# A new order for batch 0's prologue, attention of batch 1 two pieces later, and a later gate on batch 3's loads

## The chip, the cores and the metric

One core of a Trainium2 chip. Times are device microseconds (us) of one execution, medians of several. "Span" is the time of the profiled execution from its first to its last instruction; it is about 2 us shorter than the device time. Engines: PE is TensorE, PEld its weight loads, DVE is VectorE, ACT is ScalarE, POOL is GpSimd, SP is SyncE (SPq its queue of DMA issues). L571 is line 571 of that kernel; the changed kernel's lines are off by one here and there.

## The reference

Attention with projected keys and values (8 batches, 8 heads, 1024 positions, head size 64, 64 projected positions), then a maxout of two products, then an output product.

```python
k_proj = np.einsum('ks,bhsd->bhkd', E, k)
v_proj = np.einsum('ks,bhsd->bhkd', F, v)
scores = scale * np.matmul(q, k_proj.transpose(0, 1, 3, 2))
scores = scores - np.max(scores, axis=-1, keepdims=True)
attn = np.exp(scores)
attn = attn / (np.sum(attn, axis=-1, keepdims=True) + 1e-09)
attn_out = np.matmul(attn, v_proj).astype(np.float32)
x = attn_out.transpose(0, 2, 1, 3).reshape(B * S, H * D)
h1 = x @ w1; h2 = x @ w2
return (np.maximum(h1, h2) @ w_out).astype(np.float32)
```

## The kernel before

It uses max(h1, h2) = relu(x (w1 - w2)) + x w2. So it needs wd = w1 - w2 ("up" products, with a relu), m = w2 w_out (from transposes of w2, `step_w2t`, and `step_m`), and "down" products of the relu with w_out and of x with m. A batch is two units. From the second batch on, up and down products are cut into seven smaller products each (sums and differences of blocks), and each down product into pieces, between which the attention of later batches is placed. `at_slot(key, step)` hangs a step on a place in that list: ("P", unit, product, piece), ("U", unit, half, product) or ("G", unit, half).

The parts that the change and the argument touch:

```python
    def step_kv(t, h0=0, h1=H, which="kv", att=False, dma=False):   # projection of k and v
        # ... matmuls ...
        if both:                      # which == "v": batch 0's v
            eng = nc.scalar.copy if att else nc.vector.tensor_copy
            eng(out=t["vp"][:, h0:h1], in_=zd(kv_ps[:, 0:n]))
        # ...
    def step_kpt_dma(t):              # transposes projected k, issued by SyncE
        nc.sync.dma_start_transpose(
            out=t["kpt"], in_=t["kp"].rearrange("p h r d -> p (h r d)")
        )

    def step_gate(t, n, *at):         # GpSimd waits here for a tile, then issues the next loads
        nc.gpsimd.tensor_copy(out=junk, in_=t[n][(slice(0, 1), *at, slice(0, 1))])

    def step_qt_dma(t, h0=0, h1=H):   # transposes q, issued by SyncE
        nc.sync.dma_start_transpose(
            out=t["qt"][:, h0:h1].rearrange("q h (i p) -> q (h i) p", p=128),
            in_=t["q"][:, h0:h1].rearrange("p h c d -> p (h c d)"),
        )
    # ... prologue, batch 0, second group of four heads ...
    step_inv(t, 0, 1)
    warm(4)
    step_qt(t, 4, 4, 0, NI // 2)
    step_qt(t, 4, 4, NI // 2, NI)
    warm(2)
    step_sc(t, 1, 0)
    step_sc(t, 1, 1)
    step_kv(t, 0, 4, "v")
    step_dn(t, 1, 0)
    step_at(t, 0, 0)
    step_dn(t, 1, 1)
    step_at(t, 0, 1)
    step_inv(t, 1, 0)
    step_kv(t, 4, 8, "v", True)
    step_inv(t, 1, 1)
    step_wd(0, 0, 2)
    step_at(t, 1, 0, True)
    u0, u1 = [*up_slots(t, 0)], [*up_slots(t, 1)]
    step_wd(0, 2, 4)
    step_at(t, 1, 1, True)
    for u in u0, u1:
        for x in u[0:2]:
            x(r1=2)                   # first halves of four up products
    # ... slots: second halves, further w2 transposes (wt), wd blocks, step_m ...

    t = tiles[2]                      # batch 2
    at_slot(("P", 0, 1, 0), new_attn, t)
    at_slot(("P", 0, 1, 0), step_qt_dma, t, 0, H // 2)
    at_slot(("U", 1, 0, 1), step_kv, t, 0, H, "kv", True)
    at_slot(("U", 1, 0, 4), step_kpt, t, 0, H, True)
    at_slot(("G", 1, 0), step_qt_dma, t, H // 2, H)
    at_slot(("U", 1, 0, 6), step_gate, t, "qt", H // 2 - 1)
    at_slot(("U", 1, 0, 6), loads, 3, "k", "v", "q")

    for b in range(3, B):             # batches 3 to 7
        t = tiles[b]
        n = 2 * b - 3
        key = ("G", n, 0) if b == 3 else ("U", n - 1, 1, 5)
        at_slot(key, new_attn, t)
        at_slot(key, step_qt_dma, t, 0, H // 2)
        at_slot(key, step_qt_dma, t, H // 2, H)
        at_slot(("U", n, 0, 1), step_kv, t, 0, H, "kv", True, True)   # issues step_kpt_dma
        # ... gates and loads of batch b + 1 ...
```

The softmax here doesn't subtract the row's maximum and nothing guards it: scores larger than these inputs give would overflow.

Of the kernel before, what the change touches and what calls it, by code (L numbers as in the profile page):

```python
# [16 lines left out]
def kernel(  # L17
# [161 lines left out]

    def step_kv(t, h0=0, h1=H, which="kv", att=False, dma=False):  # L180
        kv_ps = att_banks()[:, 0, :] if att else mm_bank()
# [18 lines left out]
        if both:  # L200
            eng = nc.scalar.copy if att else nc.vector.tensor_copy
            eng(out=t["vp"][:, h0:h1], in_=zd(kv_ps[:, 0:n]))
        elif "v" in which:
            def finish_v():
                nc.vector.tensor_copy(out=t["vp"][KP:128, h0:h1], in_=zd(kv_ps[KP:128, 0:n]))
                if dma:
                    nc.vector.tensor_copy(out=kp[:, :, 1, :], in_=kp[:, :, 0, :])
                    step_kpt_dma(t)
                nc.vector.tensor_copy(out=fl(t["vp"][0:KP]), in_=fl(t["vp"][KP:128]))

            if att:
                return finish_v
            finish_v()
# [112 lines left out]

    def step_at(t, g, j, att=False):
        if "xt" not in t:
            new_xt(t)
        ld = t.pop(("ld", g, j))  # L330
        if att:
            both = att_banks()
            at_ps = [both[:, o, :] for o in range(2)]
        else:
            at_ps = [mm_bank() for _ in range(2)]
        values_into(t, g, j, at_ps)
        for o in range(2):
            nc.vector.tensor_tensor(
                out=x_out(t, g, j)[:, :, o, :],
                in0=at_ps[o].rearrange("q (z n) -> q z n", z=2),  # L340
                in1=ld[:, o, None, :].broadcast_to([128, 2, W]),
                op=ALU.mult,
            )
# [91 lines left out]

    def step_w2t(f0):
        ps_t = mm_bank(FP16)
        for f in range(2):
# [11 lines left out]
    def step_m(r):  # L450
        m_ps = mm_bank(n=(1, 2, 0, 3)[r])
        for fb in range(NFB):
# [170 lines left out]
    def down_steps(u, alone):  # L623
# [51 lines left out]

        def keep_d(bank):
            return keep("pd", bank, *([nc.vector.tensor_copy] if u["n"] == 0 else []))

        size = 2 * (NG + NX) // (1 if alone else 2 if u["n"] == 0 else 3)
# [7 lines left out]
        def p1():  # L687
            st["s1"] = keep_d(whole(1, "X", xbank))

# [3 lines left out]
        def p6():  # L693
            st["u1"] = keep_d(whole(6, "X", None))

        def p5():
            st["s5"] = keep_d(whole(5, "Z", ybank))

        def p7():
            st["u2"] = keep_d(whole(7, "X", None))  # L700
            if alone:
                add(1, 1, st["u2"], st["s5"])
# [49 lines left out]
    step_inv(t, 0, 1)  # L752
    warm(4)
    step_qt(t, 4, 4, 0, NI // 2)
    step_qt(t, 4, 4, NI // 2, NI)
    warm(2)
    step_sc(t, 1, 0)
    step_sc(t, 1, 1)
    step_kv(t, 0, 4, "v")
    step_dn(t, 1, 0)  # L760
    step_at(t, 0, 0)
    step_dn(t, 1, 1)
    step_at(t, 0, 1)
    step_inv(t, 1, 0)
    step_kv(t, 4, 8, "v", True)
    step_inv(t, 1, 1)
    step_wd(0, 0, 2)
    step_at(t, 1, 0, True)
    u0, u1 = [*up_slots(t, 0)], [*up_slots(t, 1)]
    step_wd(0, 2, 4)  # L770
    step_at(t, 1, 1, True)
    for u in u0, u1:
        for x in u[0:2]:
            x(r1=2)


# [5 lines left out]
    def loads(b, *names):  # L782
# [16 lines left out]
    slots = [  # L799
        (0, lambda: u0[0](r0=2)), (1, lambda: u0[1](r0=2)), (None, lambda: loads(1, "v", "q", "k")),  # L800
        (2, lambda: u1[0](r0=2)), (3, lambda: u1[1](r0=2)),
        (None, wd[1]), (4, u0[2]), (None, wt[0]), (5, u0[3]),
        (None, wd[2]), (None, wt[1]), (6, u1[2]), (7, u1[3]), (None, wt[2]), (None, wt[3]), (8, u0[4]), (9, u0[5]), (None, wd[3]),
        (10, u1[4]), (11, u1[5]), (12, u0[6]), (13, u0[7]),
# [8 lines left out]
    for n, key in enumerate(units):  # L813
# [6 lines left out]
        ups = [*up_steps(U[units[n + 1]])]  # L820
        for h, (x, y) in enumerate(((5, 1), (1, 2)) if n == 1 else ((2, 2), (2, 3))):
            slots += pieces[:x]
# [27 lines left out]
    for n, x in enumerate((  # L850
        "", "", "kv", "", "kpt", "qt00 qt10", "", "sc00 sc10", "qt01", "qt11", "",
        "dn00 in00 dn10 in10", "", "", "at00 AT10 sc01",
    )):
        key = ("P", 0, (n - 1) // 2, (n - 1) % 2) if n else (0, 19)
        for name in x.split():
# [18 lines left out]
    t = tiles[2]  # L874
    at_slot(("P", 0, 1, 0), new_attn, t)
    at_slot(("P", 0, 1, 0), step_qt_dma, t, 0, H // 2)
    at_slot(("U", 1, 0, 1), step_kv, t, 0, H, "kv", True)
    at_slot(("U", 1, 0, 4), step_kpt, t, 0, H, True)
    at_slot(("G", 1, 0), step_qt_dma, t, H // 2, H)
    at_slot(("U", 1, 0, 6), step_gate, t, "qt", H // 2 - 1)  # L880
    at_slot(("U", 1, 0, 6), loads, 3, "k", "v", "q")
# [22 lines left out]
    for n, (b, o) in enumerate(units):  # L904
        u = U[b, o]

        if b == 0:
            where = ()
        elif n == 2:
            where = (("P", 1, 0, 2), 0), (("P", 1, 1, 0), 1), (("P", 1, 1, 1), 2), (("U", 1, 0, 1), 3)  # L910
        else:
            where = tuple((("U", n - 2, 1, k), i) for k, i in ((6, 2), (3, 0), (4, 1), (5, 3)))
# [49 lines left out]
```

## Time and profile before

| | before |
|---|---|
| device time, median of 6 runs | 325.81 us (325.12 to 327.21) |
| span of the profiled execution | 323.2 us |
| PE, DVE, ACT, POOL busy | 316.0, 236.8, 203.1, 41.6 us |

PE is busy 98% of the span: only its waits can be won. The prediction shows the lines on which it rests. Those of the stage that also belong here are GpSimd's and SyncE's timelines around batch 3's loads, in the kernel before. Columns: start, duration, engine, line, what it does, and in brackets how long the engine was idle before it and what ended that.

```profile
71.82 0.61 POOL L238 COPY junk<-qt_sb 1x1 f16<-1x1 f16 x1 [19.08 <-DMA qt_sb<-q_sb]
73.04 0.90 POOL L102 DMA_DIRECT2D k_sb<-in_k_dram  x1 [0.62 <-PE mm_ps L571]
83.40 0.87 POOL L102 DMA_DIRECT2D v_sb<-in_v_dram  x1 [9.46 <-DMA qt_sb<-q_sb]
84.27 0.88 POOL L102 DMA_DIRECT2D q_sb<-in_q_dram  x1
```

```profile
100.17 5.70 SPq L258 DMA_TRANSPOSE qt_sb<-q_sb  x2
105.96 0.53 SPq L664 DMA_DIRECT2D out_dram<-o_sb  x1
106.97 1.20 SPq L232 DMA_TRANSPOSE kpt_sb<-kp_sb  x1
```

The first fence: the gate passes at 71.82, when batch 2's first q transpose has landed, and k's load goes out at 73.04. v and q go out 10 us later, since v's load itself waits for the second q transpose (the bracket says so). The second fence: q has landed at 84.27 + 15.8 = 100.07 (15.8 is the tile view's time from issue to landing), SyncE's queue then issues q's two transposes, a store, and the transpose of projected k (`kpt_sb`). This lands 2.7 us after its issue, at 109.7; PE's scores of batch 3 want it at 110.2.

### The profile page before, as it was taken

Reading aid. Unit: us, or ns where it says so; the run is one execution under the profiler, and the core shown is the slowest. Engines: PE = TensorE matmul, PEld = TensorE weight load, DVE = VectorE, ACT = ScalarE, POOL = GpSimd, SP = SyncE. Lnnn points to the kernel's source line nnn. Section 1 sums busy time; section 2 is a strip of 40 time slices with the busy share of each in tenths; the row PEclk is TensorE's granted clock in tenths of the full one; section 3 lists DMA queues with packets and bytes.
Section 4 is the critical chain, followed back from the end, with each engine's and each line's share of the span. In section 5 each row is a group of like instructions: output and inputs, shape, how many; then the busy total and the mean of one; then the engine's idle time right before and its main releaser. Section 6 shows DMA issues by size and latency. Waiting matters only on the chain.

```text
span 323.2 us, 9033 instructions
## 1 busy us (share of the span) xinstructions
PE 316.0 (98%) x3852; PEld 248.4 (77%) x3852; DVE 236.8 (73%) x420; ACT 203.1 (63%) x364; POOL 41.6 (13%) x65
## 2 busy tenths in 40 slices
PE   8989999999999999999999999999999999999995
PEld 3554457878887888878887888878887888888884
DVE  1365798896867797877967796977967796969572
ACT  1466532667676777667776777657776777764541
POOL 8649002001200300030000300030000000000000
PEclk9999999999999999999999999999999999999999
DMA  8999999999999799699979999689969130312133
GB/s 160 207 196 185 204 204 204 207 203 179 256 216 213 135 203 244 143 177 144 234 147 201 154 211 231 115 180 183 232 130 213 38 100 32 99 34 98 34 121 108
DMA packets 76280, 53.14 MB, mean 164 GB/s; under 512 B 29520, under 2 KB 76112, under 8 KB 76240
## 3 DMA queue, kind: packets, MB, share of 16 engines
q0 software_dynamic: 30976, 28.31, 56.0%
q1 hardware_dynamic: 45264, 24.25, 31.2%
q8 instruction: 30, 0.49, 0.6%
q14 instruction: 10, 0.08, 0.1%
HBM read 57.15 MB, written 16.78 MB: 229 GB/s over the span
## 4 chain that ended last, share of the span: by engine, by line
PE 84%; DMA 9%; DVE 2%; POOL 2%; issue 1%; SPq 1%; ACT 0%; DVEq 0%; POOLq 0%
PE mm_ps L649 43%; PE mm_ps L571 24%; PE att_ps L188 4%; DMA v_sb<-in_v_dram 4%; DMA qt_sb<-q_sb 3%; PE mm_ps L415 3%; PE att_ps L287 3%; PE mm_ps L275 3%; PE mm_ps L453 2%; DMA big<-in_moe_w_dram 2%; POOL q_sb L102 1%; POOL k_sb L102 1%; DVE gt_sb L586 1%; PE mm_ps L246 1%; PE mm_ps L440 1%
## 5 line engine op out<-in xcount | busy, mean ns | idle before, releaser
L542 ACT COPY p_sb<-mm_ps 128x512 f32<-128x512 f32 x172 | 97.2, 594 | 42.0 <-PE mm_ps L571 30.0
L649 PEld LDWEIGHTS <-big 128*128 128x128 f16 x768 | 73.5, 98 | 12.0 <-issue 3.5
L649 PE MATMUL mm_ps<-T_sb,big 128*128 128x256 f16 x576 | 77.9, 273 | 0.0
L586 DVE TENSOR_TENSOR gt_sb<-mm_ps,p_sb 128x512 f16<-128x512 f32 x56 | 38.6, 688 | 45.5 <-PE mm_ps L571 42.7
L571 PE MATMUL mm_ps<-big,big 128*128 128x256 f16 x336 | 50.4, 273 | 0.0
L571 PEld LDWEIGHTS <-big 128*128 128x128 f16 x448 | 43.8, 98 | 5.2
L649 PEld LDWEIGHTS <-gt_sb 128*128 128x128 f16 x384 | 35.8, 98 | 9.9 <-issue 5.4
L649 PE MATMUL mm_ps<-wo_sb,gt_sb 128*128 128x256 f16 x256 | 43.0, 273 | 0.1
L571 PEld LDWEIGHTS <-wd_sb 128*128 128x128 f16 x336 | 32.9, 98 | 3.8
L571 PE MATMUL mm_ps<-xt_sb,wd_sb 128*128 128x256 f16 x224 | 33.6, 273 | 0.0
L364 ACT ACTIVATE ex_sb<-mm_ps 128x512 f16<-128x512 f32 x50 | 27.2, 597 | 10.2 <-PE att_ps L287 8.1
L390 DVE TENSOR_TENSOR xt_sb<-att_ps,ld_sb 128x1024 f16<-128x1024 f32 x26 | 31.7, 1219 | 0.1
L673 DVE TENSOR_TENSOR o_sb<-mm_ps,p_sb 128x512 f32<-128x512 f32 x32 | 21.9, 685 | 7.7 <-PE mm_ps L649 7.7
L649 PE MATMUL mm_ps<-m_sb,xt_sb 128*128 128x256 f16 x128 | 24.4, 273 | 0.0
L238 POOL COPY junk<-qt_sb 1x1 f16<-1x1 f16 x6 | 1.7, 284 | 169.6 <-DMA qt_sb<-q_sb 169.6
L621 ACT ACTIVATE gt_sb<-mm_ps 128x512 f16<-128x512 f32 x28 | 16.8, 600 | 8.7 <-PE mm_ps L571 8.7
L532 DVE TENSOR_TENSOR big<-gt_sb 128x1024 f16<-128x1024 f16 x32 | 21.9, 685 | 0.3
L589 DVE TENSOR_SCALAR gt_sb<-gt_sb 128x512 f16<-128x512 f16 (+1 forms) x56 | 20.4, 365 | 1.9
L649 PE MATMUL mm_ps<-wo_sb,big 128*128 128x256 f16 x128 | 21.5, 273 | 0.0
L649 PE MATMUL mm_ps<-T_sb,gt_sb 128*128 128x256 f16 x128 | 21.5, 273 | 0.0
L649 PEld LDWEIGHTS <-xt_sb 128*128 128x128 f16 x192 | 18.8, 98 | 2.2
L586 DVE TENSOR_TENSOR gt_sb<-p_sb 128x512 f16<-128x512 f32 x28 | 19.1, 682 | 0.0
(88 smaller groups left out, 429.5 us busy)
## 6 DMA issues: line engine op xcount, KB each, us to landing
out_dram<-o_sb SPq DMA_DIRECT2D x63, 256.0 KB, 2.7
k_sb<-in_k_dram POOLq DMA_DIRECT2D x7, 1024.0 KB, 11.3
v_sb<-in_v_dram POOLq DMA_DIRECT2D x7, 1024.0 KB, 16.7
q_sb<-in_q_dram POOLq DMA_DIRECT2D x5, 1024.0 KB, 22.8
q_sb<-in_q_dram POOLq DMA_DIRECT2D x4, 512.0 KB, 19.4
big<-in_moe_w_dram POOLq DMA_DIRECT2D x12, 128.0 KB, 8.6
k_sb<-in_k_dram POOLq DMA_DIRECT2D x4, 256.0 KB, 6.1
q_sb<-in_q_dram POOLq DMA_DIRECT2D x4, 256.0 KB, 7.2
```

The costliest lines, as they stand in the source:

```text
L188: nc.tensor.matmul(out=kv_ps[r * KP : (r + 1) * KP, 0:n], lhsT=eft[:, i, c, :], rhs=t[w][:, h0:h1, c, :], start=(c == 0), stop=(c == NC - 1),)
L275: nc.tensor.matmul(out=banks[e][pos : pos + Z, h * W : (h + 1) * W], lhsT=t["kpt"][o * D : (o + 1) * D, head, s * Z : (s + 1) * Z], rhs=t[ ...
L364: nc.scalar.activation(out=t["ex", g, j][:, e, :], in_=banks[e], func=ACTF.Exp, scale=scale)
L390: nc.vector.tensor_tensor(out=x_out(t, g, j).rearrange("q z o n -> q o z n"), in0=at_ps.rearrange("q o (z n) -> q o z n", z=2), in1=ld[:, ...
L532: nc.vector.tensor_tensor(out=S(i), in0=x, in1=y, op=op)
L542: copy(out=x, in_=bank)
L571: nc.tensor.matmul(out=bank[:, m * W : (m + 1) * W], lhsT=w_[:, n_, (2 * d + m) * 128 : (2 * d + m + 1) * 128], rhs=a[:, n_, :], start=(n ...
L586: nc.vector.tensor_tensor(out=c_blk(j, c), in0=two(x), in1=two(y), op=ALU.add)
L589: nc.vector.tensor_scalar_max(ap, ap, 0.0)
L621: nc.scalar.activation(out=out, in_=in_, func=ACTF.Relu)
L649: nc.tensor.matmul(out=bank[:, i * CH : (i + 1) * CH], lhsT=a(c)[:, i * 128 : (i + 1) * 128], rhs=w_(c), start=(n is not None and m == (lo ...
L673: nc.vector.tensor_tensor(out=o_sb, in0=two(x), in1=two(y), op=ALU.add)
```

## The change

Its intent: in batch 0, do work while the loads of v and w1 are awaited (v's first projection between the two scores, 16 transposes of w2 before the third up product, four warm-up matmuls out); move batch 1's attention two pieces later so that its loads are there; let ScalarE instead of VectorE keep unit 0's partial results; and let batch 2's second q transpose finish before batch 3's loads start.

```diff
@@ step_kv: engine of the copy given by the caller
-            eng = nc.scalar.copy if att else nc.vector.tensor_copy
-            eng(out=t["vp"][:, h0:h1], in_=zd(kv_ps[:, 0:n]))
+            copy(out=t["vp"][:, h0:h1], in_=zd(kv_ps[:, 0:n]))
@@ step_at: a step between its two multiplications; step_w2t: may use the attention's banks (cut)
@@ step_m
-        m_ps = mm_bank(n=(1, 2, 0, 3)[r])
+        m_ps = mm_bank(n=(3, 0, 1, 2)[r])
@@ down_steps, for p1, p6, p5, p7 alike
-        def keep_d(bank):
-            return keep("pd", bank, *([nc.vector.tensor_copy] if u["n"] == 0 else []))
-            st["s1"] = keep_d(whole(1, "X", xbank))
+            st["s1"] = keep("pd", whole(1, "X", xbank))
@@ prologue
-    warm(4)
     step_qt(t, 4, 4, 0, NI // 2)
     step_qt(t, 4, 4, NI // 2, NI)
     warm(2)
     step_sc(t, 1, 0)
+    step_kv(t, 0, 4, "v")
     step_sc(t, 1, 1)
-    step_kv(t, 0, 4, "v")
+    step_at(t, 0, 0)
     step_dn(t, 1, 0)
-    step_at(t, 0, 0)
+    step_at(t, 0, 1, between=lambda: step_wd(0, 0, 2))
     step_dn(t, 1, 1)
-    step_at(t, 0, 1)
+    step_kv(t, 4, 8, "v", copy=nc.scalar.copy)
     step_inv(t, 1, 0)
-    step_kv(t, 4, 8, "v", True)
+    step_at(t, 1, 0, True)
     step_inv(t, 1, 1)
-    step_wd(0, 0, 2)
-    step_at(t, 1, 0, True)
...
             x(r1=2)
+    step_w2t(0, True)
...
         (0, lambda: u0[0](r0=2)), (1, lambda: u0[1](r0=2)), (None, lambda: loads(1, "v", "q", "k")),
+        (None, lambda: step_w2t(256, True)),
         (2, lambda: u1[0](r0=2)), (3, lambda: u1[1](r0=2)),
-        (None, wd[1]), (4, u0[2]), (None, wt[0]), (5, u0[3]),
-        (None, wd[2]), (None, wt[1]), (6, u1[2]), ...
+        (None, wd[1]), (4, u0[2]), (5, u0[3]),
+        (None, wd[2]), (6, u1[2]), ...
@@ pieces of unit 1 around its groups
-        for h, (x, y) in enumerate(((5, 1), (1, 2)) if n == 1 else ((2, 2), (2, 3))):
+        for h, (x, y) in enumerate(((6, 1), (1, 1)) if n == 1 else ((2, 2), (2, 3))):
@@ batch 1's attention: two empty places put in front
-        "", "", "kv", "", "kpt", "qt00 qt10", ...
+        "", "", "", "", "kv", "", "kpt", "qt00 qt10", ...
@@ batch 2
-    at_slot(("P", 0, 1, 0), new_attn, t)
-    at_slot(("P", 0, 1, 0), step_qt_dma, t, 0, H // 2)
+    at_slot(("P", 0, 2, 0), new_attn, t)
+    at_slot(("P", 0, 2, 0), step_qt_dma, t, 0, H // 2)
...
-    at_slot(("U", 1, 0, 6), step_gate, t, "qt", H // 2 - 1)
+    at_slot(("U", 1, 0, 6), step_gate, t, "qt", H - 1)
     at_slot(("U", 1, 0, 6), loads, 3, "k", "v", "q")
```

More of the change, by code (lines that the diff above doesn't have):

```diff
@@ L177, in new_attn, with step_kv @@
         t["qt"] = qtp.tile([128, H, HALF], FP16, tag="qt", name="qt_sb")
-    def step_kv(t, h0=0, h1=H, which="kv", att=False, dma=False):
+    def step_kv(t, h0=0, h1=H, which="kv", att=False, dma=False, copy=nc.vector.tensor_copy):
         kv_ps = att_banks()[:, 0, :] if att else mm_bank()
@@ L325, in step_inv, with step_at @@
         nc.scalar.activation(out=ld, in_=ld, func=ACTF.Exp, scale=-1.0)
-    def step_at(t, g, j, att=False):
+    def step_at(t, g, j, att=False, between=None):
         if "xt" not in t:
@@ L337, in step_at @@
         for o in range(2):
+            if o and between is not None:
+                between()
             nc.vector.tensor_tensor(
@@ L434, in step_wd, with step_w2t @@
         )
-    def step_w2t(f0):
-        ps_t = mm_bank(FP16)
+    def step_w2t(f0, att=False):
+        ps_t = att_banks(FP16)[:, 0, :] if att else mm_bank(FP16)
         for f in range(2):
@@ L693, in p6 @@
         def p6():
-            st["u1"] = keep_d(whole(6, "X", None))
+            st["u1"] = keep("pd", whole(6, "X", None))
         def p5():
-            st["s5"] = keep_d(whole(5, "Z", ybank))
+            st["s5"] = keep("pd", whole(5, "Z", ybank))
         def p7():
-            st["u2"] = keep_d(whole(7, "X", None))
+            st["u2"] = keep("pd", whole(7, "X", None))
             if alone:
@@ L800 @@
         (0, lambda: u0[0](r0=2)), (1, lambda: u0[1](r0=2)), (None, lambda: loads(1, "v", "q", "k")),
+        (None, lambda: step_w2t(256, True)),
         (2, lambda: u1[0](r0=2)), (3, lambda: u1[1](r0=2)),
-        (None, wd[1]), (4, u0[2]), (None, wt[0]), (5, u0[3]),
-        (None, wd[2]), (None, wt[1]), (6, u1[2]), (7, u1[3]), (None, wt[2]), (None, wt[3]), (8, u0[4]), (9, u0[5]), (None, wd[3]),
+        (None, wd[1]), (4, u0[2]), (5, u0[3]),
+        (None, wd[2]), (6, u1[2]), (7, u1[3]), (None, wt[2]), (None, wt[3]), (8, u0[4]), (9, u0[5]), (None, wd[3]),
         (10, u1[4]), (11, u1[5]), (12, u0[6]), (13, u0[7]),
@@ L850 @@
     for n, x in enumerate((
-        "", "", "kv", "", "kpt", "qt00 qt10", "", "sc00 sc10", "qt01", "qt11", "",
+        "", "", "", "", "kv", "", "kpt", "qt00 qt10", "", "sc00 sc10", "qt01", "qt11", "",
         "dn00 in00 dn10 in10", "", "", "at00 AT10 sc01",
     )):
-        key = ("P", 0, (n - 1) // 2, (n - 1) % 2) if n else (0, 19)
+        key = ("P", n // 15, (n - 1) // 2 % 7, (n - 1) % 2) if n else (0, 19)
         for name in x.split():
@@ L909 @@
         elif n == 2:
-            where = (("P", 1, 0, 2), 0), (("P", 1, 1, 0), 1), (("P", 1, 1, 1), 2), (("U", 1, 0, 1), 3)
+            where = (("P", 1, 1, 1), 0), (("P", 1, 1, 2), 1), (("P", 1, 2, 0), 2), (("U", 1, 0, 1), 3)
         else:
```

## The prediction

> **What bounds the kernel now.** I read the page first: its busy shares, its slices, then the chain that ended last.
>
> ```profile
> PE 316.0 (98%) x3852; PEld 248.4 (77%) x3852; DVE 236.8 (73%) x420; ACT 203.1 (63%) x364; POOL 41.6 (13%) x65
> PE   8989999999999999999999999999999999999995
> PE 84%; DMA 9%; DVE 2%; POOL 2%; issue 1%; SPq 1%; ACT 0%; DVEq 0%; POOLq 0%
> ```
>
> TensorE (PE) is busy 316.0 of 323.2 us, so no change that leaves its matmuls alone can win more than about 7 us. Its idle time lies in the first slices and at the end; the end (final add and store) isn't touched. The DMA share of the chain tells where PE waits for data. The chain in order of time, 5 to 30 us:
>
> ```profile
> 8.35 12.82 DMA v_sb<-in_v_dram
> 21.17 0.29 issue
> 21.46 5.01 DMA big<-in_moe_w_dram
> 26.47 0.47 issue
> 26.94 0.70 DVE wd_sb L431
> 27.64 0.05 issue
> 27.69 1.04 PE mm_ps L415 x4
> ```
>
> So the prologue ends on a load: the second half of v, then the last quarter-block of w1 (the tile view gives 5.4 us from its issue at 21.46, so it lands at 26.86), then one subtraction, then the third up product at 27.69. From 27.69 on the matmul starts follow each other without a gap worth naming (switches of tile shape cost 0.1 to 0.2 us each and are in both kernels), except once. The timeline of PE, 16 to 24 us and at 82 us:
>
> ```profile
> 15.57 1.04 PE L148 MATMUL mm_ps<-ones 128*128 128x512 f16 x4
> 18.43 0.41 PE L275 MATMUL att_ps<-qt_sb,kpt_sb 64*32 64x256 f16 x16 [0.16 <-DVE qt_sb L251]
> 18.78 1.06 PE L188 MATMUL mm_ps<-v_sb,eft 128*64 128x256 f16 x16
> 20.36 0.41 PE L287 MATMUL mm_ps<-ex_sb,vp_sb 64*32 64x256 f16 x16 [0.29 <-DVE vp_sb L202]
> 21.22 1.06 PE L188 MATMUL att_ps<-v_sb,eft 128*64 128x256 f16 x16
> 22.75 0.63 PE L287 MATMUL att_ps<-ex_sb,vp_sb 64*32 64x256 f16 x32 [0.47 <-ACT vp_sb L202]
> 23.80 4.92 PE L415 MATMUL mm_ps<-xt_sb,wd_sb 128*128 128x512 f16 x20 [0.42 <-DVE wd_sb L431]
> 82.88 0.41 PE L275 MATMUL mm_ps<-qt_sb,kpt_sb 64*32 64x256 f16 x16 [0.31 <-DMA qt_sb<-q_sb]
> ```
>
> The reader should see four small bracketed waits before 24 us, one more hidden in "4.92 x20" (20 matmuls of 512 columns need 20 x 0.216 = 4.32, so 0.6 is waiting, about half of it for wd at 27.69), and one at 82.88 us. The times 18.78 and 21.22 aren't free: v's first half was issued at 7.59 and took 11.1 us, so it landed at 18.69, and the second landed at 21.17.
>
> **What the Trainium skill says.** "TensorE: Matmul & The Clock Gate", section "Step-by-step: what each phase is for", gives 55.6 ns between starts at 128 columns and about 216 ns at 512. The trace agrees: 16 transposes take 32.04 to 32.94 (56 ns each), 32 matmuls of 512 columns take 6.91 us in the chain (216 ns each). The same page, "What's actually happening", says the clock drops only after an idle window of about 3.4 us; no wait here is near that, and the granted clock is 1.00 in every window I read. "DMA: Bandwidth & Descriptors", section "Issuing engines are not separate DMA queues", says transfers started by different engines run on the same 16 DMA engines and interleave. The trace agrees: the q transpose issued at 66.67 landed in 5.1 us, the one issued at 72.17, with a 1 MB k load issued 0.9 us after it, took 10.7 us.
>
> **The change part by part.**
>
> (a) Four warm-up matmuls at 15.57 go: 0.86 us of PE. But v's first projection now comes after only one block of scores and can't start before 18.7. PE gets there at about 17.4 instead of 18.78 and waits some 1.3 us. Worth nothing.
>
> (b) The second scores of the group move behind that projection. PE: projection 18.77 to 19.77, scores to 20.11; the copy of vp by VectorE (DVE) is done at 20.30 as before, so the wait of 0.29 shrinks, but the values start at 20.36 as before. The exponentials of the moved scores start at 20.25 instead of about 19.3 and take 1.02 (its row at 62.26), so the last sums start at 21.3, and the second projection of v at about 21.64 instead of 21.22. Its copy on ScalarE (ACT) ends at 23.1, the last values start at 23.17 (22.75 before). The first up matmul then starts at about 23.73 (23.80 before: there wd was awaited, and wd is now made one VectorE place earlier).
>
> (c) Two blocks of eight w2 transposes (8 x 0.056 = 0.45 us each) go from behind the 27.69 mark to before it. PE: four half products (8 x 0.216 = 1.73) to 25.46, transposes to 25.91, two halves to 26.77, transposes to 27.22, two halves to 28.08. So the third product starts at 28.08 and not 27.69, but 0.90 us of later work is already done: net 0.90 - 0.39 = 0.51 us won. wd for it is ready at 27.63 as before, so the load is no longer the bound. Had PE been ready by 27.69, the win would be 0.90.
>
> (d) From there PE is continuous, and everything shifts 0.5 us earlier if its data are there. I checked each floor. wd's third block landed at about 30.8 and is subtracted by 31.6; it is wanted at 32.4. w_out landed at 26.72 + 11.3 = 38.0; wanted at 39.3. v of batch 1 landed at 28.64 + 19.5 = 48.1, and the kernel before used it at 48.15, with no slack. A PE 0.5 us earlier would have stopped there. Moving batch 1's attention two pieces later (2 x 6 matmuls x 0.109 = 1.3 us) takes it to about 48.9. This part wins nothing by itself; it keeps the 0.5.
>
> (e) Unit 0's four partial results: VectorE 684 ns each, 2.7 us off an engine that is 86 to 91% busy from 40 to 70 us; ScalarE takes 594 ns each, 2.4 us, where it is only about 30% busy up to 60 us. PE didn't wait for VectorE there, so 0 on the path, but slack.
>
> (f) The gate on batch 3's loads now waits for the second q transpose. That leaves the transpose almost alone: issued at about 72.2, landed at about 77.5 instead of 82.83, wanted at about 82. The wait at 82.88 goes: the gap between starts there was 0.47 against 0.09 at the same switch elsewhere, so 0.38 us won. Batch 3's k goes out at about 77.6 instead of 73.04, v and q earlier than their 83.40; its use is at 102.74.
>
> Sum: 0.51 + 0.38 = 0.9 us off 325.81, so 324.9 us.
>
> **The rivals.**
>
> First, the load is the bound after all and PE is ready by 27.69. For it: my chain in (b) adds several latencies of 0.05 to 0.2 us, and being 0.3 too slow in it is easy. Against it: the moved exponentials really are on the way to the second projection. It would make 0.9 + 0.4 = 1.3 us, 324.5 us.
>
> Second, a new wait eats the win. In (b) v between the scores makes PE wait for the exponentials (about 0.4 us at 20.9 to 21.3), and if ScalarE, which now also has the w2 copies (1.01 us each) ahead of the relus, frees a PSUM bank late, the products at 29 to 31 us stall. I reckon the relus end 0.3 to 0.5 us before their banks are wanted, which is thin. Or w2's second transposes wait for the accumulator bank that VectorE frees at about 26.6 (PE comes at 26.77). Either would leave a win of 0.2 to 0.4 from the gate alone: 325.5 us.
>
> Third, batch 3's loads, all issued after the transpose, land late or collide with the next transposes at 100 us. In favour: the DMA share was high throughout that stage (1.03 to 1.29 of 16 engines from 50 to 90 us). Against: v and q leave some 5 us earlier than before, k has 25 us. It would cost a wait of up to 1 us near 102: 325.8 us.
>
> Fourth, the attention moved later runs into the scores of the next group, whose banks it shares: 1.75 us of pieces and 0.55 of attention lie between, and VectorE needs about 1.8. Thin, but 0.5 us at most.
>
> **Range and chances.** The middle is 324.9. The first rival puts the low edge near 324.2, runs differ by 0.4 us either way (325.14 to 325.97), so 324.0; rivals two to four put the high edge at the time of before, 325.8. A change of 2% is 6.5 us: more than PE's whole idle time in the stages touched (about 3 us, plus 0.86 of warm-up), so faster than that is next to impossible; slower by that would need a serial stall that no part of this shows. Chances 0.01, 0.98, 0.01.
>
> **What would show it.** Right: PE waits 1.2 to 1.4 us before the first v projection at about 18.77; the second one starts at 21.5 to 21.7; the third up product starts at 27.7 to 28.2 with 16 transposes before it; batch 1's k and v projection at 48.5 to 49; the second q transpose takes about 5 us and no DMA wait stands at 82 us; the PE busy time falls by about 0.9 us (the warm-ups). The span shrinks by 0.9 us, half of it before 30 us. Wrong: a wait for ScalarE in front of the products at 29 to 31 us, a DMA wait at 39, 49 or 102 us, or a third product later than 28.6.

## The result, and the profile after

| | before | after |
|---|---|---|
| device time, median of 6 runs | 325.81 us | 330.44 us |
| lowest to highest | 325.12 to 327.21 | 328.56 to 336.3 |
| span of the profiled execution | 323.2 us | 326.8 us |
| ratio of fast runs, 95% interval | | 1.013 [1.0088, 1.0172] |

A ratio here is the mean time of one kernel's fast runs over the mean of the other's in the same rounds, so it isn't quite the ratio of the medians quoted. The 336.3 us run was slow (granted clock 0.985) and is left out of the ratio. The profiled run (328.56 us) was a fast one. Within the 2% band the kernel counts as the same; in fact it is 1.3% slower, 4 to 5 us, outside the predicted range.

The page after, in two of the views that the prediction opened with: busy times and PE's 40 slices.

```profile
PE 315.1 (96%) x3848; PEld 248.2 (76%) x3848; DVE 234.8 (72%) x416; ACT 205.3 (63%) x368; POOL 41.3 (13%) x65
PE   8969999999999599999999999999999999999995
```

PE's busy time fell by 0.9 us, as predicted, yet its share fell from 98 to 96%: it waits more. Slice 14 of 40 (each 8.2 us, so 106 to 114 us) shows a 5 where the kernel before has a 9. PE's timeline of the changed kernel, at the places that the prediction named and in that slice:

```profile
19.20 1.06 PE L188 MATMUL mm_ps<-v_sb,eft 128*64 128x256 f16 x16 [1.72 <-DMA v_sb<-in_v_dram]
22.10 1.06 PE L188 MATMUL mm_ps<-v_sb,eft 128*64 128x256 f16 x16
24.18 1.90 PE L416 MATMUL mm_ps<-xt_sb,wd_sb 128*128 128x512 f16 x8
25.92 0.61 PE L441 MATMUL att_ps<-ident,big 128*128 128x128 f16 x8
27.23 0.61 PE L441 MATMUL att_ps<-ident,big 128*128 128x128 f16 x8
27.68 2.54 PE L416 MATMUL mm_ps<-xt_sb,wd_sb 128*128 128x512 f16 x11
76.14 0.60 PE L572 MATMUL mm_ps<-xt_sb,wd_sb 128*128 128x256 f16 x4 [0.18 <-ACT ex_sb L365]
82.98 0.41 PE L274 MATMUL mm_ps<-qt_sb,kpt_sb 64*32 64x256 f16 x16
110.09 0.40 PE L286 MATMUL att_ps<-ex_sb,vp_sb 64*32 64x256 f16 x16
113.92 0.41 PE L274 MATMUL mm_ps<-qt_sb,kpt_sb 64*32 64x256 f16 x16 [3.43 <-DMA kpt_sb<-kp_sb]
```

The row at 113.92 holds the loss. PE waited 3.43 us for the transpose of batch 3's projected k. In the kernel before the same scores follow the same values without a wait:

```profile
109.99 0.40 PE L287 MATMUL att_ps<-ex_sb,vp_sb 64*32 64x256 f16 x16
110.21 0.62 PE L275 MATMUL mm_ps<-qt_sb,kpt_sb 64*32 64x256 f16 x16
```

At the values the two kernels are 0.10 us apart, at the scores 113.92 - 110.21 = 3.71 us, at the end of the span 3.6 us. So nearly all of the difference of these two traces lies in this one wait. It also means that none of the predicted 0.9 us is there at 110 us: the changed kernel is 0.10 us behind. The wait at 82.9 us is gone as intended (no bracket at 82.98), but a new one stands at 76.14 (0.18 us by its bracket, on ScalarE's exponentials, at the shifted pieces). From start to start it costs more: 0.78 us from the four matmuls at 75.36 to this row, where four such take 0.44, so 0.34 us.

Why is the transpose late? GpSimd's and SyncE's timelines of the changed kernel, to be held against those of before:

```profile
79.57 0.18 POOL L237 COPY junk<-qt_sb 1x1 f16<-1x1 f16 x1 [25.57 <-DMA qt_sb<-q_sb]
80.80 0.90 POOL L102 DMA_DIRECT2D k_sb<-in_k_dram  x1 [1.05 <-PE mm_ps L572]
81.68 0.88 POOL L102 DMA_DIRECT2D v_sb<-in_v_dram  x1
82.55 0.90 POOL L102 DMA_DIRECT2D q_sb<-in_q_dram  x1
```

```profile
105.54 4.65 SPq L257 DMA_TRANSPOSE qt_sb<-q_sb  x2
110.28 0.67 SPq L665 DMA_DIRECT2D out_dram<-o_sb  x1
111.05 1.23 SPq L231 DMA_TRANSPOSE kpt_sb<-kp_sb  x1
```

k goes out 7.8 us later than before; v and q go out 1.7 us earlier. But the three now run one behind the other, and q, the last, lands 22.9 us after its issue, at 82.55 + 22.9 = 105.45 instead of 100.07. SyncE issues in its program's order: q's transposes wait for q until 105.54, and the store and k's transpose stand behind them. k's transpose is issued at 111.05 instead of 106.97 and lands 2.8 us later, at 113.85. PE starts at 113.92. What k's transpose itself needs was not late. VectorE's last copy of projected k, first in the kernel before, then in the changed one:

```profile
106.62 0.28 DVE L207 COPY kp_sb<-kp_sb 64x512 f16<-64x512 f16 x1
106.73 0.28 DVE L206 COPY kp_sb<-kp_sb 64x512 f16<-64x512 f16 x1
```

So it was ready at 106.9 and 107.0. In the kernel before the transpose was issued at once, in the changed one 4.0 us later: that is the time it stood behind q's transposes and the store.

The DMA view shows what the later gate leaves unused. Each row is 72 to 82 us in 40 slices of 0.25 us, the busy share of the DMA engines in tenths; first the kernel before, then the changed one:

```profile
DMA  9999999999999999689999979237799999999999
```

```profile
DMA  9999999999999999999994000000000000000009
```

The second q transpose has moved its last byte at about 77.5 us. The gate sees it landed at 79.5 (72.71 + 6.8), and the first load is issued at 80.80. For 4.2 us, to about 81.7, next to nothing is moved, where the kernel before was loading k. The first data then are those of stores.

The traces also hold every single DMA packet (the DMA view sums them; the times that follow were read from the records). The second q transpose's 256-byte packets start from 74.68 to 77.45 in the changed kernel and from 74.27 to 77.86 in the kernel before. So in this trace k's load, issued at 73.04, had little part in how fast these data went: its own first packet came only at 77.26, when they were nearly through. What came late was the transpose's completion. From 77.9 to 79.7 the kernel before moved k's packets alone (queue, packets, MB, share of the 16 engines; q0 has GpSimd's loads),

```profile
q0 software_dynamic: 148, 0.15, 80.0%
```

and the transpose was seen landed at 82.83, 5.0 us after its last packet (2.1 in the changed kernel). Of the 3.9 us by which the time from issue to landing fell (10.7 to 6.8), 2.9 are this, and 1.0 is the data's. In the changed kernel k's first packet moves at 82.82, 5.6 us later than the 77.26 of before, and this is what q's landing shows, 5.4 us later. Other traces with the old gate mix data and completion otherwise: in x1_gate_half, below, the transpose's last packet starts at 79.74, among k's.

### The profile page after: what moved, and what is told of

Same layout as the page of the kernel before. It is cut to its first block, busy times and chain, and to the rows that moved or that the text cites. A ratio compares the mean times of both kernels' runs of the same rounds, so it can differ in the third digit from the quotient of the medians.

```text
span 326.8 us, 9028 instructions
## 1 busy us (share of the span) xinstructions
PE 315.1 (96%) x3848; PEld 248.2 (76%) x3848; DVE 234.8 (72%) x416; ACT 205.3 (63%) x368; POOL 41.3 (13%) x65
## 4 chain that ended last, share of the span: by engine, by line
PE 89%; DMA 4%; DVE 2%; POOL 2%; issue 1%; ACT 1%; SPq 0%; DVEq 0%; POOLq 0%
PE mm_ps L650 45%; PE mm_ps L572 26%; PE mm_ps L416 4%; PE att_ps L188 4%; DMA v_sb<-in_v_dram 4%; PE att_ps L286 3%; PE mm_ps L274 3%; PE mm_ps L454 2%; POOL q_sb L102 1%; DMA kpt_sb<-kp_sb 1%; POOL k_sb L102 1%; DVE gt_sb L587 1%; PE mm_ps L188 1%; PE mm_ps L245 1%; DVE xt_sb L391 0%
## 5 line engine op out<-in xcount | busy, mean ns | idle before, releaser
L543 ACT COPY p_sb<-mm_ps 128x512 f32<-128x512 f32 x176 | 99.6, 593 | 44.3 <-PE mm_ps L572 29.9
## 6 DMA issues: line engine op xcount, KB each, us to landing
q_sb<-in_q_dram POOLq DMA_DIRECT2D x5, 1024.0 KB, 22.9
```

The source lines that it names most:

```text
L543: copy(out=x, in_=bank)
```

## The experiments

Two theories were set against each other first. **The gate** (called G in the expectations): the later gate delays batch 3's loads and so causes the wait at 114 us and the whole loss. Its rival: the new prologue, the shifted pieces or the copies' new engine are to blame, and the wait at 114 is only where it shows. A third came up later, called T: part of the loss is a clock that falls while PE waits.

### First round: the gate alone

**x1_gate_half**: the changed kernel with the old gate.

```diff
-    at_slot(("U", 1, 0, 6), step_gate, t, "qt", H - 1)
+    at_slot(("U", 1, 0, 6), step_gate, t, "qt", H // 2 - 1)
```

> The changed kernel with only the gate put back to the first q transpose of batch 2. Theory G (the gate holds batch 3's k load back until the second transpose has landed, the DMA engines idle meanwhile, q of batch 3 lands 5 us later, and with it the transposes and the scores at 114 us): batch 3's k load goes out at about 73.5 and not 80.8, its q lands at about 100 and not 105.5, no stall over 0.3 us at 110 to 114, time 325.0 to 326.0, all runs at a granted clock of 1.0. Rival S (the later attention and the shifted pieces fill the queue of SyncE, so that the transposes come late whatever the gate does): the stall of 3 us or more stays, 328 us or more. Rival P (part of the loss sits in the prologue): 326.5 to 327.5 with the stall at 114 gone.

Measured: 325.31 us (325.1 to 325.55), ratio to before 0.9979 [0.9942, 1.0017]. Undoing one index takes the whole loss away. GpSimd's, SyncE's and PE's rows for k, k's transpose and the scores:

```profile
73.70 0.90 POOL L102 DMA_DIRECT2D k_sb<-in_k_dram  x1 [1.05 <-PE mm_ps L572]
108.18 1.23 SPq L231 DMA_TRANSPOSE kpt_sb<-kp_sb  x1
110.85 0.41 PE L274 MATMUL mm_ps<-qt_sb,kpt_sb 64*32 64x256 f16 x16 [0.39 <-DMA kpt_sb<-kp_sb]
```

k is out at 73.70, q lands at 101.5, and the wait is 0.39 us instead of 3.43. That a wait stays says how thin the margin at this place is, even with the old gate.

**x2_before_gate_full**: the kernel before with the new gate, and nothing else.

```diff
-    at_slot(("U", 1, 0, 6), step_gate, t, "qt", H // 2 - 1)
+    at_slot(("U", 1, 0, 6), step_gate, t, "qt", H - 1)
```

> The kernel before with only the gate moved to the second q transpose. Theory G: the DMA wait of 0.3 us at 82.9 goes, batch 3's q lands at 105 or later, a stall of 3 to 4 us before the scores at 110 us, time 328.3 to 330.5 and a wider scatter than before. Rival S: no stall, 325.4 us, a little faster than before.

Measured: 329.88, 331.02, 330.07 us, ratio 1.0134 [1.0094, 1.0175]: the one index alone makes the kernel before as slow as the changed one. The profiled execution of this kernel took 1819 us, with matmuls of 256 columns at about 1.04 us each; that isn't explained, its trace isn't used, and the three timed runs decide.

**x3_q_first**: the changed kernel, new gate, with q loaded first.

```diff
-    at_slot(("U", 1, 0, 6), loads, 3, "k", "v", "q")
+    at_slot(("U", 1, 0, 6), loads, 3, "q", "k", "v")
```

> The changed kernel with batch 3 loaded in the order q, k, v in place of k, v, q; gate as changed. Theory G in its form that only q's place as the last of three loads matters: the transposes start before 100 us and the stall at 110 goes, but v, now last, lands at about 105, so PE stalls 2 to 3 us at the k and v projection at 102.8 instead; time 327.5 to 329. If the three loads together did not need the time that I think (about 25 us from the first issue), neither stall would show and the time would be about 325.

Measured, in two runs: 327.30 and 327.36 us, a little under the range expected, ratio 1.0042 [0.9995, 1.009]. SyncE's q transposes start at 100.14 (105.54 in the changed kernel), k's is issued at 109.73, and the scores follow the values at 112.57, with 0.19 us of waiting at most (on PEld's row). The wait has moved to v, the load that now comes last:

```profile
104.98 0.38 PE L188 MATMUL att_ps<-v_sb,eft 128*64 128x512 f16 x1 [1.67 <-DMA v_sb<-in_v_dram]
```

Some load is last whatever the order, and each order had its own wait. As a test of the chain's middle this run is weak. q landed early, but its transposes, beside the loads of k and v, took 8.86 us to issue, and k's transpose landed at 112.53 (109.73 + 2.8): a PE on time, at 110.2, would have waited for it all the same. That q's late landing held up k's transpose is read from SyncE's queue and from projected k being ready at 107.0; no run was made with k's transpose issued ahead of q's.

**x4_fill**: the changed kernel with 16 matmuls of 512 columns (3.5 us) on unused data just before batch 3's scores. If the wait there is real, they fit into it and cost nothing.

```diff
+            if t is tiles[3] and (g, j) == (0, 0):
+                for _ in range(16):
+                    nc.tensor.matmul(
+                        out=banks[0], lhsT=ones16[:, 0:128], rhs=ones16, start=True, stop=True
+                    )
             score(t, g, j, banks)
```

> The changed kernel with 16 needless matmuls of 512 columns (3.45 us) in front of the first scores of batch 3, where PE waits 3.4 us, into the bank that the scores then overwrite. Theory T: the scatter of the changed kernel (328.6 to 336.3, granted clock 0.985 to 1.0) comes from that long idle time, after which the clock is sometimes granted lower. Then this kernel has a clock of 1.0 in every run, and times of 328.3 to 329.3 with a spread under 0.8 us. If the scatter has another cause, the times spread over 3 us or more as those of the changed kernel did.

Measured: 329.6, 329.17, 329.57 us, ratio 1.0108 [1.007, 1.0145]. The matmuls cost nothing. The spread of 0.4 us is what T expects; two of the times lie above its range, and one clock was 0.995. This kernel's profiled execution was odd too (654.5 us, PE slow throughout, though the record of the granted clock says 1.0 as in x2_before_gate_full) and isn't used; the kernel was run again as x10_fill_again.

### Second round: can the gate's gain be had without its cost, and does the prologue gain?

**x5_before_again**: the kernel before, profiled again, to see which of its times repeat.

> The kernel before, profiled once more. The question is when v's first half lands, which in the changed kernel's profile is 19.1 us and in that of before 18.7, though nothing up to then differs but PE's warm-ups. If that is chance of a run: between 18.7 and 19.3 here. If the changed kernel makes it late: 18.6 to 18.8. Time 325.0 to 326.2.

Measured: 326.34 us, span 324.6 us. v's first half landed at 18.6 us (18.69 in the first profile). In the profiles of the changed kernel and its variants it lands at 18.1 to 19.2, on both sides of that, so the 19.2 of the changed kernel's own profile looks like the spread of that load and not like an effect of the order; two profiles of the kernel before are few. In this trace PE also waited 0.70 us for F at 7.2 us, the clock fell to 0.50 from 8.05 to 11.46, and PE came to v's first projection at 20.78 instead of 18.78; the first profile lacks all this. Differences of half a microsecond in the prologue can't be read from single traces.

**x6_k_early**: the new gate, but batch 3's k goes out ahead of it.

```diff
-    at_slot(("U", 1, 0, 6), loads, 3, "k", "v", "q")
+    at_slot(("P", 0, 6, 0), loads, 3, "k")
+    at_slot(("U", 1, 0, 6), loads, 3, "v", "q")
```

> The changed kernel with batch 3's k load issued before the gate (right after batch 1's last q transposes on PE, some 58 us), its v and q after the gate, which stays at the second q transpose. Theory G says that the loss is the k load held behind the gate: k then lands by 78, v and q go out at about 80 and q lands at 96 to 99, no stall at 110 to 114, time 324.8 to 325.6, so below the run with the gate at half. If k's early load delays the first q transpose of batch 2, a DMA wait of up to 2 us stands before the scores at 75 us, and the time is 326 to 327.5.

Measured: 329.39 us (328.91 to 329.68), ratio 1.0107 [1.0077, 1.0138]. The main expectation fell. k went out at 59.83 and was still moving when batch 2's first q transpose was issued at 67.33; that took 10.6 us to land instead of about 5, and PE waited for it:

```profile
77.97 0.41 PE L274 MATMUL mm_ps<-qt_sb,kpt_sb 64*32 64x256 f16 x16 [2.91 <-DMA qt_sb<-q_sb]
```

The load that is taken away from the second transpose falls upon the first. The expectation had named this as its alternative, with less than it cost. One reason is in the clock's record: after this wait it was 0.50 for 3.41 us, about 1.7 us of work (an estimate, half of 3.41), and 2.9 + 1.7 accounts for the 4.6 us by which this trace's span of 327.8 exceeds the 323.2 of before. PE doesn't wait before batch 3's scores, but that doesn't show the late chain mended: q landed at 102.84, not at 96 to 99, k's transpose at 114.4, and PE came there only at 114.74 because it had lost 4.5 us by then.

**x7_v_old_order**: x1_gate_half with v and the values in the old order (the w2 transposes before the third up product stay).

```diff
-    step_kv(t, 0, 4, "v")
     step_sc(t, 1, 1)
-    step_at(t, 0, 0)
+    step_kv(t, 0, 4, "v")
     step_dn(t, 1, 0)
-    step_at(t, 0, 1, between=lambda: step_wd(0, 0, 2))
+    step_at(t, 0, 0)
     step_dn(t, 1, 1)
-    step_kv(t, 4, 8, "v", copy=nc.scalar.copy)
+    step_at(t, 0, 1, between=lambda: step_wd(0, 0, 2))
     step_inv(t, 1, 0)
+    step_kv(t, 4, 8, "v", True, copy=nc.scalar.copy)
```

> The run with the gate at half (x1), with v's projections and the values put back to their order of before; the w2 transposes stay in the waits and wd one place earlier. Theory O (the prediction's step b: putting v between the scores holds PE for the exponentials and gives away about 0.4 us of what the w2 transposes win): the second v projection starts 0.4 us after the second half of v could be used or less, the third up product comes 0.3 to 0.5 us earlier than in x1 (28.50 there), time 0.3 to 0.5 us under x1, 324.8 to 325.1. Rival: the new order of v is what wins, and this run is as slow as before, 325.7.

Measured: 325.17 us (324.57 to 331.05, the last a slow run and left out of the ratio), ratio 0.9974 [0.9941, 1.0007]. Against x1_gate_half (325.31) no difference can be told. The traces do differ, and v's first half landed at 19.2 in both: the second v projection starts at 21.50 and the first up product at 23.61, against 22.05 and 24.14 in x1_gate_half. At the third up product 0.17 us of that is left (28.33 against 28.50), not the 0.3 to 0.5 expected.

**x8_both**: x6_k_early and x7_v_old_order together (both edits as above, with the new gate).

> Old order of v and early k together (x6 and x7), the version that should beat both kernels: 324.3 to 325.0, 0.3 to 0.4 percent under before, no stall over 0.4 us after 30 us.

Measured: 329.09 us (328.67 to 330.79), ratio 1.0109 [1.0071, 1.0147], with a PE wait of 3.31 us on the first q transpose at 78.04, and the clock at 0.50 after it. It says again what x6_k_early says, and misses the 324.3 to 325.0 expected.

### Third round: the clock, and the prologue alone

**x9_after_again**: the changed kernel, unedited. **x10_fill_again**: x4_fill, unedited. Theory T says that the idle time before batch 3's scores lets the granted clock fall in some executions, which the filler prevents.

> The changed kernel again, beside its filled twin on one chip. Its first runs spread from 328.6 to 331.4, one more at 336.3, with granted clocks of 1.0 down to 0.985. Theory T (PE's idle 3.5 us at 110 sometimes lets the granted clock fall): median 329.3 to 330.5, spread of the fast runs 1.5 us or more. If that scatter was the chip's of that hour: 328.5 to 329.2, spread under 1 us.

> The same with the needless matmuls in the wait (as x4). Theory T: median 328.4 to 329.4, at least 0.7 us under the changed kernel of the same rounds, spread under 1 us. If idle PE has nothing to do with it: the same median as the changed kernel, or up to 0.3 us more.

Measured: x9_after_again 330.24 us (328.83 to 331.64), ratio 1.0141 [1.0111, 1.017]; x10_fill_again 329.39 us (329.09 to 330.39), ratio 1.0117 [1.0095, 1.0139]. The spread of x10_fill_again's runs, 1.3 us, is more than the 1 us that T expected. In the profiled execution of x9_after_again the wait was 4.16 us, up to 114.46. The windows view after it, 116 to 120 us (columns: length, then busy time and instructions of PE, PEld, DVE, ACT, POOL, then PE's granted clock, DMA share, GB/s), first x9_after_again, then x10_fill_again, and as a third row x8_both after its wait at 78 us:

```profile
116.00:120.00 4.00, 4.00 (x21) 2.82 (x19) 0.00 (x0) 2.43 (x5) 0.35 (x1) 0.50 1.08 156
116.00:120.00 4.00, 4.00 (x39) 3.59 (x38) 2.78 (x5) 2.93 (x7) 0.00 (x0) 1.00 1.15 182
78.50:81.50 3.00, 3.00 (x16) 2.08 (x16) 0.00 (x0) 2.94 (x6) 0.00 (x0) 0.50 1.18 339
```

The clock column fell to 0.50 in the one and stayed at 1.00 in the other; from 116 to 120 us PE began 21 matmuls in the one and 39 in the other. The Trainium skill, "TensorE: Matmul & The Clock Gate", section "What's actually happening", gives half clock after an idle window of about 3.4 us, and says that the window runs freely. Two traces fit that: 4.16 us idle, then 0.50; and 3.43 us idle in the first profile of the changed kernel, with 1.00 throughout. Others don't: the clock also fell to 0.50 after waits of 2.91 (x6_k_early) and 3.31 us (x8_both), and in the prologue after 0.70 (x5_before_again, the kernel before) and 0.54 us (x3_q_first). Each of these four falls lasted 3.41 us, the one in x9_after_again 6.83, twice that. So a fall after a wait is shown here; that it needs 3.4 us of idle time is not. The wait costs 3.7 us and, where the clock fell, 2.6 us more: x9_after_again is 0.54 us behind the first profile at the scores (114.46 against 113.92) and 3.16 us behind at the same matmuls later (123.11 against 119.95). Of the five fast runs of the changed kernel in its first timing, the two above 331 us had a mean granted clock of 0.987 and 0.99, the three below 330 us 0.995 to 1.0 (one fall of 3.41 us takes 0.005 off the mean). So it explains part of the spread, and why its median lies 4.6 us above the one before while its profiled run, with the clock at 1.00, lies 2.8 us above. The difference of the two medians, 0.85 us, fits T, but the two ratios' intervals overlap; the clock column is the direct evidence.

**x11_old_order_again**: x7_v_old_order, unedited, to narrow its interval.

> The best kernel so far (x7: gate at half, v in its old order) once more, to see whether its 0.26 percent under the kernel before holds: 324.6 to 325.4, ratio 0.996 to 0.999.

Measured: 325.64 us (324.54 to 330.57, the last a slow run), ratio 0.9983 [0.9957, 1.001]. No gain over before is shown. Its trace has a gap of 1.36 us before the scores at 83.92, where batch 2's second q transpose came late.

**x12_prologue_only**: the kernel before with the prologue, the w2 transposes and the order of step_m's banks of the changed one. Attention places, pieces, partial results and gate stay as before (the diff is the first part of the change's, without `keep` and without all that stands after `slots`).

> The kernel before with the new prologue alone (order of v, wd earlier, w2 transposes in the waits, the banks of the m products); attention of batch 1, its pieces, the partial results and the gate as before. The prediction's steps c and d: the prologue wins 0.3 to 0.5 us at the w2 transposes, but PE then comes to batch 1's k and v projection before v has landed (28.8 + 19.5 = 48.3 us) and waits 0.3 to 0.8 us there with a DMA wait in the trace, so 325.4 to 325.9, no gain worth naming. If v lands early enough: no wait at 48 us and 325.2 to 325.4.

Measured: 324.66 us (324.31 to 325.56), before in the same rounds 325.98 (324.58 to 326.85), ratio 0.9971 [0.9949, 0.9993]. With 325.4 to 325.9 expected, it came out lower. It is the only one of the study's twelve ratios whose interval lies below 1, and the lowest: about 0.9 us, or 0.3%. Its trace (span 323.5, not shorter than 323.2) doesn't show where that would come from in full. PE was late in its first 12 us (the first transposes of projected k start at 11.48, in the kernel before at 9.78), so that it came to v's first half only at 19.04, after its landing at 18.1. Batch 1's projection starts at 47.94 instead of 48.15, so 0.2 us is won by then, and then the wait at 83 us takes it back:

```profile
83.10 0.41 PE L274 MATMUL mm_ps<-qt_sb,kpt_sb 64*32 64x256 f16 x16 [0.74 <-DMA qt_sb<-q_sb]
```

In the kernel before this row stands at 82.88 with 0.31. A PE that comes earlier waits longer here, as long as the transpose's landing doesn't move (it took 12.0 us in this trace, 10.7 before). With twelve ratios looked at, an interval that ends at 0.9993 is no strong proof of a gain.

## Why the prediction was wrong

By its own steps:

- **(a) Warm-ups, worth nothing.** PE's busy time fell by the predicted 0.9 us, and PE waited 1.72 us (predicted about 1.3) for v's first half, which landed at 19.2 instead of 18.7. Right.
- **(b) v between the scores.** Predicted 21.64 for the second projection and 23.73 for the first up product; the trace has 22.10 and 24.18, both 0.45 late. That is v's late landing (0.5), so the step's chain of latencies was right. What it compared this with was not: the 23.80 of before includes a wait for wd, which the change makes earlier in either order. With v's landing alike, the old order starts the first up product 0.53 us sooner (x7_v_old_order against x1_gate_half; 23.44 to 23.65 in the three traces of the old order, 24.05 to 24.18 in the four of the new one where PE was on time), of which 0.17 is left at the third; in the times no difference is shown.
- **(c) 16 transposes before the third up product.** It was predicted at 28.08. In the trace, the row at 27.68 begins with the four matmuls that end the first four products (4 x 0.216 = 0.86), so the third starts at 28.54; worked out alike it starts at 28.33 in x7_v_old_order and at 28.38 in x12_prologue_only. With 0.90 us of transposes already done, the win at this point (27.69 + 0.90 less these) is 0.05 us in the changed kernel's profile and 0.26 and 0.21 in the others, not 0.51. The step's own sum held: from the first up product to the third the trace has 4.36 us, the prediction 4.35. The 0.46 us missing in the changed kernel's profile is (b)'s 0.45, handed on. (The prediction also read 0.6 us of waiting out of "4.92 x20", half of it for wd. The row's length includes the end of the last matmul; from start to start, 23.80 to 28.56, it is 0.44, all of it the wait for wd at 27.69. The sum doesn't use it.)
- **(d) The floors.** That batch 1's v would stop an earlier PE was not seen: x12_prologue_only, without the two-piece shift, started the projection at 47.94 without a DMA wait, v having landed at 28.56 + 18.9 = 47.46. The 19.5 us of the first trace was one draw of a load time that varies (18.9 to 19.9 in the traces used). In the changed kernel the projection starts at 49.41 without a wait, 0.4 us after the 48.5 to 49 predicted, as (b) was.
- **(e) Partial results by ScalarE.** VectorE's busy time fell by 2.0 us and ScalarE's rose by 2.2; none of PE's waits read here goes back to it. It was not tried alone, and neither was the shift of the pieces, whose new wait at 76.14 costs 0.34 us from start to start (x12_prologue_only, without these two parts, has no wait there). With 0.05 won in (c), 0.38 at 82.9 and 0.34 lost here, the changed kernel would be 0.09 us ahead at 110 us; it is 0.10 behind, so about 0.2 us of loss isn't traced.
- **(f) The gate: this step failed, with the third rival that belongs to it.** What it wanted came: the wait at 82.9 is gone. But the transpose, predicted to land at about 77.5, landed at 79.5; only its data were through at 77.5, and in the kernel before they were so at 77.9, so the later gate mostly freed its completion. "Batch 3's k goes out at about 77.6" left out the way from the last byte to the next load: landing seen at 79.5, load out at 80.80, its first packet at 82.82 (77.26 before). And "v and q leave some 5 us earlier than before" compared times of issue, not of landing: they left 1.7 us earlier, behind a k that left 7.8 us later, and q landed 5.4 us later. The step looked for the loads' first use in the projection at 102.74 ("k has 25 us"), where there is indeed no wait. The use that had no slack is q's: SyncE issues k's transpose behind q's transposes, and in the kernel before that transpose landed at 109.7 for scores at 110.2. The wait overlooked is thus that of batch 3's scores for k's transpose, 3.43 us where the step had none; undoing the gate alone (x1_gate_half) and making it alone (x2_before_gate_full) show that the gate causes the loss. In the third rival, "a wait of up to 1 us near 102" should have been some 3.7 us at 110: k's transpose landed 113.85 - 109.7 = 4.15 us later, less 0.5 of slack, 3.65; 3.71 lies between the two traces' starts. (q's 5.4 us became 4.15, since k's transpose was issued 6.8 us after q's in the kernel before and 5.5 us after in the changed one.)

The first rival (load bound, 324.5), the second (a new wait in the prologue) and the fourth (attention running into scores) aren't what happened; the 0.18 us at 76.14 is the nearest to them. The prediction also said of the clock page that the clock drops only after about 3.4 us of idling and that no wait was near that. The change made one, and the clock then fell in one of the two profiled executions of the changed kernel; but it fell after shorter waits too, once in the kernel before (x5_before_again).

What stays open: how much of the prologue's gain is real (x12_prologue_only's 0.3% against its trace), and what parts (e) and the piece shift do alone; and whether issuing k's transpose ahead of q's would let the later gate keep its gain.

## What to carry to other kernels

When a wait is moved ahead of a group of loads, work out the landing of the last of them, not the issue of the first, and follow it through every queue that issues in order: here q's load held a transpose queue, and the work behind it that needed something else was what came late. Before a load is held back to clear the way for another transfer, see in the packets whether that transfer's data are slowed, or only reported late: the time from issue to landing doesn't tell them apart. A DMA queue that is kept clear for one transfer stands empty until that transfer's end has been seen and the next one has started; 4.2 us of silence is dearer than a wait of 0.4 us. And look for the places where the kernel before had no slack, not only for those where it waited: a row without a bracket may have been 0.5 us from one.

## What the Trainium skill lacked or had wrong

- "DMA: Bandwidth & Descriptors", section "Latency and other measured facts", puts the fixed cost of a DMA at about 2 us, mostly the round trip of the receipt. Here the receipt was shorter: from the last packet's start to the landing of batch 2's first q transpose it took 0.5 us (71.43 to 71.91 in the changed kernel). The second one's 2.1 us (77.45 to 79.52) are a straggler: 15 of the 16 increments of its semaphore had come by 77.96. The last followed a 16 KB instruction packet that ran from 77.46 to 78.34. The same pattern stands in all four traces where batch 3's first load was held back to this landing (2.0 to 2.1 us); in x6_k_early and x8_both no instruction packet was near, and it took 0.6 us. That the packet is the cause fits, but wasn't tested.
- No page says how long a transpose takes beside a load: half of batch 2's q landed in 4.7 to 7.6 us without batch 3's k load beside it, and in 9.5 to 12.0 us with it. Nor by how much a load beside it can put off its completion when its data are through (5.0 us in the kernel before, 77.86 to 82.83).
- "Advanced Engine Details and Errata", section "X-Bar Transpose (TRN2)", expects 350 to 400 GB/s of a transpose. In stretches where almost nothing but a transpose's packets moved, the changed kernel shows 286 (70 to 71 us) and 217 GB/s (75 to 77 us).
- "TensorE: Matmul & The Clock Gate", section "What's actually happening", gives half clock after an idle window of about 3.4 us. Here it followed waits of 0.54, 0.70, 2.91, 3.31 and 4.16 us, and did not follow one of 3.43 us.
- No page has the danger of a queue that issues in order when loads land late: q's load, 5.4 us late, held up a transpose that doesn't need q and whose own data were ready, by 4.0 us.
